# Experts ranked by their count of rows, 768 slots for the last three, and the weighting of scores behind the division

## The chip, the cores and the metric

The kernel runs on one core of a Trainium2 chip. The metric is device microseconds of one execution, lower is better. Three runs of the kernel before gave a median of 543.9 us (542.6 to 544.37).

## The reference

An attention with gates (a recurrence over 768 steps, for 4 batches and 8 heads of 40) gives 3072 rows of 320 numbers. These rows go to a layer of eight experts: each row to the two experts with the highest noisy logits, with the two weights of a softmax.

```python
for t in range(S):                       # S = 768
    m_new = np.maximum(f_gate[:, :, t] + m, i_gate[:, :, t])
    f_stab = np.exp(f_gate[:, :, t] + m - m_new)
    i_stab = np.exp(i_gate[:, :, t] - m_new)
    m = m_new
    C = f_stab[:, :, None, None] * C + i_stab[:, :, None, None] * np.einsum('bhd,bhe->bhde', vt, kt)
    n = f_stab[:, :, None] * n + i_stab[:, :, None] * kt
    denom = np.maximum(np.abs(np.einsum('bhd,bhd->bh', n, qt)[:, :, None]), 1.0)
    y[:, :, t] = sigmoid(o_gate[:, :, t]) * np.einsum('bhde,bhe->bhd', C, qt) / denom
x = y.transpose(0, 2, 1, 3).reshape(3072, 320)
noisy_logits = x @ w_gate + np.log1p(np.exp(x @ w_noise)) * noise
top2 = np.argpartition(-noisy_logits, 2, axis=1)[:, :2]
top2_w = softmax of the two
for e in range(8):
    for k in range(2):
        mask = top2[:, k] == e
        h = np.maximum(x[mask] @ w1[e], 0.0)          # 320 -> 1024
        out[mask] += top2_w[mask, k, None] * (h @ w2[e])   # 1024 -> 320
```

## The kernel before

**Attention.** The recurrence is computed in 24 units, each a chunk of 64 steps for two batches, 128 rows of the result. The order of the work on each engine is written out by hand. Unit `i` issues, among others: `s_part` (scores `s`, PE), `e_part` (the weights `w` from the gates), `k_part` (DVE: `kd`, the keys scaled for the state), `p_part` (DVE: `p` = `s` times `w`, 128 x 1024), `c_part` (PE: the new state `st`, ACT copies it), `o_part` (PE: `o` from `p` and the values and state), `f_part` (DVE: the reciprocal `dn` of the denominator, its maximum, then `tm` = `o` times `dn`; POOL: `xr` = `tm` times the output gate) and `l_part`, `t_part` (PE: logits and transposes). `k_part` and `p_part` prepare unit `i + 1` while unit `i` is still in its later steps; `p` and `kd` have two buffers each.

**Routing.** Behind each group of units the two best experts of its rows, the softmax weights, and the rank of each row within its expert are computed in fp32, mostly on DVE (`g_part`: `ln`, `na`, `co`, `m`, `mi`, and `ob`, a one-hot of the rank that PE adds into a table). `fill()` puts these small instructions between the attention's, so many per call. The table `TBL` has 7 columns per expert and 128 rows: slot `t * 128 + p` of expert `e` holds a row number (or nothing), with a sign that says which of the two weights is meant. `decode` turns columns of it into row numbers `TOK` and masks `KM`. POOL gathers rows by `TOK` (`gather`) and adds results back by it (`put`).

**Experts.** Every expert has room for 832 rows: six tiles of 128 and one of 64. The matrix products are done in parts of high and low precision (`w1h`, `w1l`, `xh`, `xl`, `hh`, `hlo`, ...). The first layer (`mm1`, L931) goes over 8 chunks of 128 hidden units, for each of two halves of the rows, 448 and 384 wide for experts 2 to 7; 8 matmuls per chunk. ACT and DVE turn each chunk into `hh` and `hlo`. The last 64 rows of the first half go to `ht` (L951). The second layer (`mm2`, L960 to L962) makes 24 matmuls per tile of 128 rows; the tile of 64 rows makes 16 (L968, L969). Expert 0 is done in three parts of rows, 0 to 384, to 640 and to 832, as routing finishes, beside the end of the attention; expert 1 in parts of 512 and 320.

While one expert computes, SP loads the next one's weights (`load_w1`, `load_w2`), ACT and DVE split them into high and low, POOL gathers the next rows, DVE turns them (`turn_x`), 16 DMAs on SP spread them over the partitions (`spread_x`), and `split_x` splits them. After expert 7 a flag is read: if any expert has more than 832 rows, a branch (`tc.If(most > NT)`) works through the rest.

The loop over the experts, with the places that the change touches:

```python
for h in range(2):
    for f in range(8):
        mm1(e, h, f)
        ...
        if TURN <= 8 * h + f < TURN + 7 and e + 1 < NE:
            turn_x(8 * h + f - TURN)
            if 8 * h + f == TURN + 6:
                spread_x()
                weigh(e + 1)
xs = split_x()
for n, t in enumerate(OR1):
    put(e, t, mm2(e, t))
```

Of the kernel before, what the change touches and what calls it, by code (L numbers as in the profile page):

```python
# [31 lines left out]
FIT = 2048  # L32
# [4 lines left out]
NB = 4  # L37

# [20 lines left out]
def build(ctx, tc, qk, vk, fi, noise, wgn, w1, w2, cst, ce, out):  # L59
# [30 lines left out]
    flag = keep.tile([128, 1], I32, name="flag")  # L90
    early = ctx.enter_context(tc.tile_pool(name="early", bufs=1))
# [43 lines left out]
    def load_w1(e, ks=((0, 2), 2)):  # L135
        for k in ks:
            if k == 2:
                for p in range(2):
                    SP.dma_start(RAW1[64 * p:64 * p + 64, 2], w1[e, 256:320])
            else:  # L140
                a, b = k
                SP.dma_start(RAW1[:, a:b], w1[e, a * 128:b * 128].rearrange("(k p) f -> p k f", p=128))
# [303 lines left out]

    def decode(a, b, more=True):

        t, n = TBL[:, a:b], slice(a, b)
        V.scalar_tensor_tensor(VC[:, n], t, 0.0, cs[:, C_VAC + a:C_VAC + b], op0=OP.is_equal, op1=OP.mult)  # L450
        V.scalar_tensor_tensor(AB[:, n], t, -1.0, t, op0=OP.mult, op1=OP.max)
        V.tensor_scalar(KM[:, n, 0], t, 0.0, None, op0=OP.is_gt)
        x = AB[:, n]
        if more:
            far = rt.tile([128, b - a], F32, name=f"far{a}", bufs=1)
            V.tensor_scalar(far, x, 0.5, FIT // 2, op0=OP.mult, op1=OP.add)
            x = rt.tile([128, b - a], F32, name=f"near{a}", bufs=1)
            V.scalar_tensor_tensor(x, AB[:, n], 0.0, far, op0=OP.add, op1=OP.min)
        V.scalar_tensor_tensor(TOK[:, n], x, -1.0, VC[:, n], op0=OP.add, op1=OP.add)
        V.tensor_scalar(KM[:, n, 1], t, 0.0, None, op0=OP.is_lt)  # L460
# [24 lines left out]
    def g_part(g):  # L485
# [121 lines left out]
        if u0 + nb == NU:  # L607
# [3 lines left out]
            yield  # L611
            V.tensor_reduce(dd[:, 0:1], rk[:, 0:8], AX.X, OP.max)
# [68 lines left out]
    def parts(e):  # L681
        s = (E0S, (0, 512, NT))[e] if e < 2 else (0, CA, NT)
        return [slice(a, b) for a, b in zip(s, s[1:])]


    def load_w2(e):
        SP.dma_start(RAW2, w2[e].rearrange("(j p) c -> p j c", p=128))
# [38 lines left out]
    def tiles(e, h=None):  # L726
        if h is None:
            return range(7)
# [22 lines left out]
    while i < NU - LEAD:  # L751
# [33 lines left out]
        p_part(i + 1)  # L785
# [11 lines left out]
        f_part(i, lambda: fill(0.15, False))  # L797
        t = l_part(i)
# [93 lines left out]
    QC = (224, 224, 192, 192)  # L892
    QO = (0, 224, 448, 640)
# [8 lines left out]
    def spread_x():  # L902
# [6 lines left out]
    def split_x():  # L909
# [88 lines left out]
    def advance(much, by=1):  # L998
# [61 lines left out]
    assert done[0] == NU  # L1060
    load_w2(1)
# [8 lines left out]
    for f in range(8):  # L1070
        mm1(0, 2, f)
        if f == 5:
            next(side)
        if f in (0, 3):
            transpose_x(tiles(0, 1)[f // 3])
    for t in tiles(0, 2):
# [9 lines left out]
    for e in range(1, NE):  # L1086
# [4 lines left out]
        for h in range(2):  # L1091
            for f in range(8):
# [7 lines left out]
                if TURN <= 8 * h + f < TURN + 7 and e + 1 < NE:  # L1100
                    turn_x(8 * h + f - TURN)
                    if 8 * h + f == TURN + 6:
                        spread_x()
# [11 lines left out]
        xs = split_x()  # L1115
        for n, t in enumerate(OR1):
# [45 lines left out]
    with tc.If(most > NT):  # L1162
        V.memset(ec, 0.0)
        with tc.For_i(0, NE, 1) as e:
            weights(e)
            x = xf[0:CS, 0:RW]
            tok = m2.tile([128, 1], I32, name="ftk")
            km = m2.tile([128, 2], F32, name="fkm")
            SP.dma_start(tok[0:CS], TOK[CS:128].rearrange("p (e c) -> p e c", e=NE)[:, bass.ds(e, 1), TC - 1:TC].rearrange("p e c -> p (e c)"))
            SP.dma_start(km[0:CS], KM[CS:128].rearrange("p (e c) k -> p e c k", e=NE)[:, bass.ds(e, 1), TC - 1].rearrange("p e k -> p (e k)"))  # L1170
            P.indirect_dma_start(out=x, out_offset=None, in_=XD, in_offset=bass.IndirectOffsetOnAxis(ap=tok[0:CS], axis=0),
# [106 lines left out]
```

## Time and profile before

| | |
|---|---|
| median of three runs | 543.9 us |
| profiled execution, span | 545.7 us |
| first matmul of expert 0 | at 138.6 us |
| matmuls (PE), share of the span | 96% |
| DVE, share of the span | 66% |
| ACT, POOL | 47%, 42% |

The page shows one profiled execution: busy time of each engine, then 40 slices of the span in tenths, the DMA queues, the chain that ended last, and groups of instructions. In a row of a group stands: line, engine, operation, `out<-in` by the program's names, shape, count, busy time in us, mean duration in ns, and behind the bar the engine's idle time just before such instructions, with what ended it. PE is TensorE's matmul, PEld its weight load, DVE VectorE, ACT ScalarE, POOL GpSimd, SP SyncE (it issues DMAs here). The expert stage takes the larger part of the span: an expert of 2 to 7 takes about 47.7 us.

### The profile page before, as it was taken

To read this page: it belongs to the slowest core of one execution; us is meant where nothing else is said; L and a number is where in the kernel's file an instruction comes from. 1 tells how busy PE (TensorE), PEld (TensorE's weight loads), DVE (VectorE), ACT (ScalarE), POOL (GpSimd) and SP (SyncE) were. 2 spreads that over 40 slices of the span, in tenths; PEclk is the share of its full clock that TensorE was granted. 3 is DMA by queue.
4 is the path that set the end of the run, shared out by engine and by line. 5 is a ranking of instruction groups with operands and counts; after the bars stand their busy time and mean duration, and the time that the engine had idled before them with its cause. 6 is when DMAs were issued, how large, how long until landed. Compare 5 with 4: busy or idle time off the path is not lost.

```text
span 545.7 us, 13298 instructions
## 1 busy us (share of the span) xinstructions
PE 521.9 (96%) x5100; PEld 486.9 (89%) x5101; DVE 361.6 (66%) x983; ACT 255.1 (47%) x634; POOL 227.9 (42%) x282
## 2 busy tenths in 40 slices
PE   8889998988999899999999999999999999999995
PEld 3778887877989798999999999999999999999994
DVE  8988999998786377764854675485467548546411
ACT  8858877877614154432541543254154325415300
POOL 7445463164112837056224705632570563251043
PEclk9979999998999999999999999999999999999998
DMA  5898787897767626088159418614941771461033
GB/s 147 216 229 221 205 227 189 199 223 197 264 191 236 106 41 194 10 170 225 39 97 261 93 35 231 136 47 81 270 97 31 194 171 49 92 144 21 1 36 47
DMA packets 49797, 77.25 MB, mean 142 GB/s; under 512 B 10281, under 2 KB 39664, under 8 KB 49728
## 3 DMA queue, kind: packets, MB, share of 16 engines
q1 hardware_dynamic: 38464, 57.39, 37.9%
q0 software_dynamic: 11264, 18.95, 19.0%
q8 instruction: 42, 0.69, 0.5%
q14 instruction: 27, 0.22, 0.1%
HBM read 52.49 MB, written 17.73 MB: 129 GB/s over the span
## 4 chain that ended last, share of the span: by engine, by line
PE 73%; DVE 20%; issue 2%; DMA 1%; ACT 1%; POOL 1%; POOLq 0%; DVEq 0%; SPq 0%; ACTq 0%
PE s L931 24%; PE e L931 12%; PE o L960 5%; PE o L961 5%; PE o L962 5%; PE st L961 5%; PE st L960 4%; PE st L962 4%; DVE p L348 3%; DVE ob L602 2%; DVE kd L342 2%; DVE tm L382 1%; PE o L371 1%; PE st L969 1%; PE st L968 1%
## 5 line engine op out<-in xcount | busy, mean ns | idle before, releaser
L983 POOL DMA_INDIRECT y_out<-y,tok x56 | 92.3, 1647 | 194.8 <-DVE y L973 191.2
L940 ACT ACTIVATE hh<-s 128x384 fp32r<-128x384 f32 (+3 forms) x91 | 42.7, 470 | 83.0 <-PE s L931 80.7
L931 PE MATMUL s<-xh,w1h 128*128 128x384 f32 (+5 forms) x273 | 78.6, 345 | 0.9 <-DVE xh L743 0.8
L709 POOL DMA_INDIRECT xg<-rows,tok x56 | 63.0, 1125 | 29.2 <-issue 15.1
L931 PE MATMUL s<-xh,w1l 128*128 128x384 f32 (+5 forms) x273 | 64.3, 343 | 0.6 <-DVE xh L743 0.6
L943 DVE SCALAR_TENSOR_TENSOR hlo<-s,hh 128x384 fp32r<-128x384 f32 (+3 forms) x91 | 47.5, 522 | 20.1 <-ACT hh L940 16.6
L961 PE MATMUL o<-w2l,hh 128*128 128x320 f32 x192 | 59.8, 311 | 0.0
L960 PE MATMUL o<-w2h,hh 128*128 128x320 f32 x192 | 59.7, 311 | 0.0
L962 PE MATMUL o<-w2h,hlo 128*128 128x320 f32 x192 | 59.1, 308 | 0.0
L931 PEld LDWEIGHTS s<-xh,w1h 128*128 128x128 f32 x273 | 49.2, 188 | 4.0 <-ACT hh L940 1.0
L961 PE MATMUL st<-w2l,hh 128*128 128x320 f32 x168 | 52.3, 311 | 0.3 <-issue 0.3
L960 PE MATMUL st<-w2h,hh 128*128 128x320 f32 x168 | 52.1, 310 | 0.0
L962 PE MATMUL st<-w2h,hlo 128*128 128x320 f32 x168 | 51.7, 308 | 0.0
L931 PEld LDWEIGHTS s<-xh,w1l 128*128 128x128 f32 x273 | 48.4, 188 | 3.2 <-DVE xh L743 0.9
L931 PE MATMUL s<-xl,w1h 128*128 128x384 f32 (+5 forms) x182 | 47.6, 343 | 0.0
L383 POOL TENSOR_TENSOR xr<-tm,vk 128x320 f32<-128x320 f32 x24 | 21.3, 887 | 52.9 <-DVE tm L382 10.6
L973 DVE TENSOR_SCALAR y<-o,gw 128x320 f32<-128x320 f32 x24 | 13.2, 550 | 42.3 <-PE o L962 42.3
L931 PE MATMUL e<-xh,w1h 128*128 128x384 f32 (+5 forms) x135 | 39.6, 348 | 0.4 <-DVE ht L951 0.3
L973 DVE TENSOR_SCALAR y<-st,gw 128x320 f32<-128x320 f32 x21 | 11.6, 551 | 41.2 <-PE st L962 41.1
L940 ACT ACTIVATE hh<-e 128x384 fp32r<-128x384 f32 (+3 forms) x45 | 21.3, 473 | 34.6 <-PE e L931 24.9
L960 PEld LDWEIGHTS o<-w2h,hh 128*128 128x128 f32 x192 | 36.1, 188 | 0.3 <-DVE y L973 0.2
L962 PEld LDWEIGHTS o<-w2h,hlo 128*128 128x128 f32 x192 | 36.2, 188 | 0.0
(222 smaller groups left out, 1303.3 us busy)
## 6 DMA issues: line engine op xcount, KB each, us to landing
vk<-vk_in SPq DMA_DIRECT2D x48, 242.0 KB
raw<-w_in SPq DMA_DIRECT2D x7, 1280.0 KB
qk<-qk_in SPq DMA_DIRECT2D x48, 160.0 KB
raw<-w_in SPq DMA_DIRECT2D x7, 1024.0 KB
raw<-w_in SPq DMA_DIRECT2D x19, 256.0 KB
y_out<-zrow SPq DMA_DIRECT2D x15, 320.0 KB
xt__2782<-xb SPq DMA_DIRECT2D x24, 84.0 KB
rows<-xr POOLq DMA_DIRECT2D x12, 160.0 KB
```

What stands on the lines that cost most here:

```text
L342: V.tensor_mul(KD[u], VKS[u % 4][:, :, 328:648].rearrange("p x (h d) -> p x h d", h=H), W[u][:, :, :, L - 1:L].to_broadcast([128, 2, H, D]))
L348: V.tensor_mul(PP[u], SQ[u], W[u])
L383: P.tensor_mul(XR[u], tm.rearrange("p h d -> p (h d)"), SG[u % 4])
L709: P.indirect_dma_start(out=XG[0:rows_of(t), t], out_offset=None, in_=XD[0:n], in_offset=bass.IndirectOffsetOnAxis(ap=token(e, t), axis=0), ...
L931: T.matmul(ps[:, 0:n], l, r, start=i == 0, stop=i == len(ops) - 1)
L940: A.activation(hi, x, AF.Relu)
L943: V.scalar_tensor_tensor(lo, x, 0.0, hi.bitcast(F32), op0=OP.max, op1=OP.subtract)
L960: T.matmul(ps, HH[:, j, c], W2H[:, j], start=j == 0, stop=False)
L961: T.matmul(ps, HH[:, j, c], W2L[:, j], start=False, stop=False)
L962: T.matmul(ps, HLO[:, j, c], W2H[:, j], start=False, stop=j == 7)
L973: V.tensor_scalar(y[0:n], ps[0:n], GW[e][0:n, t:t + 1], None, op0=OP.mult)
L983: st = P.indirect_dma_start(out=out, out_offset=bass.IndirectOffsetOnAxis(ap=token(e, t), axis=0), in_=y[0:n], in_offset=None, compute_op= ...
```

## The change

There are two parts.

First, experts 2 to 7 are worked through by falling count of rows. Six experts are ranked behind the last group's ranks: `key` = 8 times the count less the expert's number, `over` compares all pairs, its sum `POS` is the rank of each, `SEL` the one-hot of rank and expert, `WHO` the expert's number at each rank. `deal` multiplies the columns of `TBL` for these experts by `SEL` and adds over the experts, so that `TBP` holds the table in the order of ranks; it is then decoded. This is spread over the chunks of expert 0's third part. Weights of the expert at a rank are addressed with a number that SP loads from `WHO` into a register. The first three by rank keep 832 slots; the last three have 768, in halves of 384 and 384, six tiles and no `ht`. The flag takes another 64 on the count of these three, and the branch for what does not fit works on up to 128 rows left over per expert.

Second, `p_part(i + 1)` no longer stands right behind `k_part(i + 1)` but behind `f_part(i)`.

```diff
+    def deal():
+        x = rt.tile([128, NR, TC, NR], F32, name="dealt", bufs=1)
+        rows_ = TBL[:, EF * TC:].rearrange("p (e t) -> p t e", e=NR)
+        V.tensor_mul(x, SEL[:, :, None, :].to_broadcast([128, NR, TC, NR]), rows_[:, None].to_broadcast([128, NR, TC, NR]))
+        yield
+        V.tensor_reduce(TBP.rearrange("p (r t) -> p r t", r=NR), x, AX.X, OP.add)
+        yield
+        yield from decode_steps(EF * TC, NE * TC, True, TBP)
...
+            V.scalar_tensor_tensor(key, held, 8.0, i8[:, EF:8], op0=OP.mult, op1=OP.subtract)
+            V.tensor_tensor(over, key[:, None, :].to_broadcast(sq), key[:, :, None].to_broadcast(sq), op=OP.is_gt)
+            V.tensor_reduce(POS, over, AX.X, OP.add)
+            V.tensor_tensor(SEL, POS[:, None, :].to_broadcast(sq), i8[:, 0:NR, None].to_broadcast(sq), op=OP.is_equal)
+            V.tensor_mul(over, SEL, i8[:, None, EF:8].to_broadcast(sq))
+                V.tensor_reduce(WHO, over, AX.X, OP.add)
+            V.tensor_scalar(key, POS, LONG - 0.5, float(CS), op0=OP.is_gt, op1=OP.mult)
+            V.tensor_add(held, held, key)
...
-        s = (E0S, (0, 512, NT))[e] if e < 2 else (0, CA, NT)
+        s = (E0S, (0, 512, NT))[e] if e < EF else (0, CA, NT) if is_long(e) else (0, NM // 2, NM)
...
+    def weights_of(e):
+        if e < EF:
+            return slice(e, e + 1)
+        if e not in whose:
+            whose[e] = nc.values_load(WHO[0:1, e - EF:e - EF + 1], engines=[mybir.EngineType.SP], min_val=EF, max_val=NE - 1,
...
+        return bass.ds(whose[e], 1)
+
+    def is_long(e):
+        return e < EF + LONG
...
-            return range(7)
+            return range(7 if is_long(e) else 6)
...
         k_part(i + 1)
-        p_part(i + 1)
         fill(0.2, False)
         s_room(i + 2)
         c_part(i)
...
         f_part(i, lambda: fill(0.15, False))
+        p_part(i + 1)
         t = l_part(i)
...
-    QC = (224, 224, 192, 192)
-    QO = (0, 224, 448, 640)
+    def quarters(e):
+        return ((224, 224, 192, 192), (0, 224, 448, 640)) if is_long(e) else ((192,) * 4, (0, 192, 384, 576))
...
-                decode(E0S[h] // 128, E0S[h + 1] // 128 if h < 2 else NE * TC)
+                decode(E0S[h] // 128, E0S[h + 1] // 128 if h < 2 else EF * TC)
...
+    while routing:
+        fill(1.0)
+    dealing = deal()
...
     for f in range(8):
         mm1(0, 2, f)
+        next(dealing, None)
...
-                if TURN <= 8 * h + f < TURN + 7 and e + 1 < NE:
+                if e + 1 < NE and 8 * h + f - TURN in tiles(e + 1):
...
-        for n, t in enumerate(OR1):
+        xs = split_x(e + 1) if e + 1 < NE else iter(())
+        for n, t in enumerate(x for x in OR1 if x in tiles(e)):
```

On DVE, in one unit of the attention (a unit in the middle, with routing between its steps; `kd` and `p` are those of the next unit), the order before is:

```order
L342 TENSOR_TENSOR kd<-vk_108,w 128x640
L348 TENSOR_TENSOR p<-s,w 128x1024
L376 RECIPROCAL dn<-o 128x8
L503 SCALAR_TENSOR_TENSOR co_1804<-t_4_1741,ue_1740 128x32
L378 SCALAR_TENSOR_TENSOR dn<-dn 128x8
L505 RECIPROCAL na_1738<-t_4_1741 128x32
L382 SCALAR_TENSOR_TENSOR tm<-dn,o 128x320
L507 TENSOR_TENSOR co_1804<-co_1804,na_1738 128x32
L509 TENSOR_TENSOR ln_1742<-ln_1742,co_1804 128x32
```

and with the change, in the same unit:

```order
L350 TENSOR_TENSOR kd<-vk_112,w 128x640
L384 RECIPROCAL dn<-o 128x8
L534 SCALAR_TENSOR_TENSOR co_1806<-t_4_1745,ue_1744 128x32
L386 SCALAR_TENSOR_TENSOR dn<-dn 128x8
L536 RECIPROCAL na_1742<-t_4_1745 128x32
L390 SCALAR_TENSOR_TENSOR tm<-dn,o 128x320
L356 TENSOR_TENSOR p<-s,w 128x1024
L538 TENSOR_TENSOR co_1806<-co_1806,na_1742 128x32
L540 TENSOR_TENSOR ln_1746<-ln_1746,co_1806 128x32
```

`p` moves over the division's three instructions and the routing between them; the routing keeps its place among the rest, and now follows `p` where it followed `tm`.

On DVE, in the third part of expert 0 with the change (`dealt` and `tbp` are the dealing; `hlo`, `ht` are chunks of the first layer; `xl`, `xh` are rows of expert 1 being split):

```order
L1011 SCALAR_TENSOR_TENSOR hlo<-e,hh 128x128
L1019 SCALAR_TENSOR_TENSOR ht<-e,ht 128x64
L487 TENSOR_TENSOR dealt<-sel,tbl 128x252
L808 TENSOR_TENSOR xl<-s_3458,xh 128x2x128
L809 TENSOR_TENSOR xh<-s_3458,xh 64x128
L1011 SCALAR_TENSOR_TENSOR hlo<-s_3465,hh 128x128
L1019 SCALAR_TENSOR_TENSOR ht<-s_3465,ht 128x64
L489 TENSOR_REDUCE tbp<-dealt 128x42
```

Of these rows L487 and L489 are new; each of the dealing's instructions stands behind one chunk's `ht` and ahead of what follows it.

On SP, the loads of an expert's weights and the spreading of its rows, before:

```order
L687 DMA raw_2777<-w_in 128x8x320
L142 DMA raw_116<-w_in 128x2x1024
L139 DMA raw_116<-w_in 64x1024 x2
L907 DMA xt__2782<-xb 32x2x224 x2
L907 DMA xt__2782<-xb 32x3x224 x2
```

and with the change:

```order
L753 DMA raw_2781<-w_in 128x8x320
L745 TENSOR_LOAD who
L150 ISA
L150 DMA raw_120<-w_in 128x2x1024
L147 ISA
L147 DMA raw_120<-w_in 64x1024
L147 ISA
L147 DMA raw_120<-w_in 64x1024
L974 DMA xt__2786<-xb 32x2x224 x2
L974 DMA xt__2786<-xb 32x3x224 x2
```

The transfers stand in the same order; a register load from `who` and the arithmetic on addresses (ISA) come ahead of them.

More of the change, by code (lines that the diff above doesn't have):

```diff
@@ L37 @@
 NB = 4
+EF, LONG = 2, 3
+NR = NE - EF
 STEP, SHARE = 0.19, 1.65
@@ L90, in build @@
     flag = keep.tile([128, 1], I32, name="flag")
+    POS = keep.tile([128, NR], F32, name="pos")
+    WHO = keep.tile([128, NR], I32, name="who")
+    SEL = keep.tile([128, NR, NR], F32, name="sel")
+    TBP = keep.tile([128, NR * TC], F32, name="tbp")
     early = ctx.enter_context(tc.tile_pool(name="early", bufs=1))
@@ L445, in bc_part, with decoding @@
             done[0] += len(b[0]) // 2
-    def decode(a, b, more=True):
[L449 to L460, printed above, removed]
+    def decoding(t, vac, tok, km, vc, ab, more, pool, name):
+        V.scalar_tensor_tensor(vc, t, 0.0, vac, op0=OP.is_equal, op1=OP.mult)
+        yield
+        V.scalar_tensor_tensor(ab, t, -1.0, t, op0=OP.mult, op1=OP.max)
+        yield
+        V.tensor_scalar(km[:, :, 0], t, 0.0, None, op0=OP.is_gt)
+        yield
+        x = ab
+        if more:
+            shape = [128, ab.shape[1]]
+            far = pool.tile(shape, F32, name=f"far{name}", bufs=1)
+            V.tensor_scalar(far, x, 0.5, FIT // 2, op0=OP.mult, op1=OP.add)
+            yield
+            x = pool.tile(shape, F32, name=f"near{name}", bufs=1)
+            V.scalar_tensor_tensor(x, ab, 0.0, far, op0=OP.add, op1=OP.min)
+            yield
+        V.scalar_tensor_tensor(tok, x, -1.0, vc, op0=OP.add, op1=OP.add)
+        yield
+        V.tensor_scalar(km[:, :, 1], t, 0.0, None, op0=OP.is_lt)
+        yield
@@ new lines, in decode_steps @@
+    def decode_steps(a, b, more=True, t=None):
+        n = slice(a, b)
+        t = TBL[:, n] if t is None else t
+        return decoding(t, cs[:, C_VAC + a:C_VAC + b], TOK[:, n], KM[:, n], VC[:, n], AB[:, n], more, rt, a)
+    def decode(a, b, more=True):
+        run(decode_steps(a, b, more))
+    def deal():
+        x = rt.tile([128, NR, TC, NR], F32, name="dealt", bufs=1)
+        rows_ = TBL[:, EF * TC:].rearrange("p (e t) -> p t e", e=NR)
+        V.tensor_mul(x, SEL[:, :, None, :].to_broadcast([128, NR, TC, NR]), rows_[:, None].to_broadcast([128, NR, TC, NR]))
+        yield
+        V.tensor_reduce(TBP.rearrange("p (r t) -> p r t", r=NR), x, AX.X, OP.add)
+        yield
+        yield from decode_steps(EF * TC, NE * TC, True, TBP)
@@ L1075, in build @@
             transpose_x(tiles(0, 1)[f // 3])
+    run(dealing)
     for t in tiles(0, 2):
```

60 lines of the change are left out of this document (43 added, 17 removed).

## The prediction

> **What bounds the kernel now.** I read the page's busy shares and slices first, then the windows by stage, then the chain that ended last, and last the timelines of the two stages that the change touches.
>
> ```profile
> span 545.7 us, 13298 instructions
> PE 521.9 (96%) x5100; PEld 486.9 (89%) x5101; DVE 361.6 (66%) x983; ACT 255.1 (47%) x634; POOL 227.9 (42%) x282
> PE   8889998988999899999999999999999999999995
> DVE  8988999998786377764854675485467548546411
> PEclk9979999998999999999999999999999999999998
> ```
>
> The reader is to see two kernels in one. In the first ten slices (the attention) both PE and DVE stand near 9 tenths; from slice 15 on (the experts) PE alone is full. The windows put numbers to it (columns: length, busy PE, PEld, DVE, ACT, POOL, then clock, DMA share, GB/s).
>
> ```profile
> 45.00:125.00 80.00, 73.45 (x1746) 65.19 (x1744) 76.39 (x236) 63.42 (x171) 37.00 (x58) 1.00 0.84 212
> 139.00:205.00 66.00, 62.92 (x439) 57.34 (x438) 44.56 (x185) 25.49 (x76) 23.77 (x28) 1.00 0.60 164
> 205.00:539.00 334.00, 333.94 (x2009) 323.99 (x2007) 189.49 (x454) 122.96 (x303) 135.96 (x146) 1.00 0.48 112
> ```
>
> From 205 to 539 us PE is idle 0.06 us in 334, at full clock: what PE is spared there, the kernel is spared. From 45 to 125 us DVE is idle 3.6 us in 80 and PE 6.55: DVE sets the pace, but PE is only 6.55 us behind it, so a faster DVE can win at most that there. The chain confirms it: in the attention it runs on DVE nearly without a break.
>
> ```profile
> 86.07 0.73 DVE kd L342
> 86.80 1.14 DVE p L348
> ...
> 88.76 2.59 DVE ob L602 x4
> ```
>
> **Part 1, the last three experts: 768 slots for 832.** PE's timeline of expert 6 before (its first half of 448 columns, its second of 384, then the tiles of the second layer):
>
> ```profile
> 442.93 0.57 PE L931 MATMUL s<-xh,w1h 128*128 128x448 f32 x2
> ...
> 456.07 0.52 PE L931 MATMUL e<-xh,w1h 128*128 128x384 f32 x2
> ...
> 467.37 0.31 PE L960 MATMUL st<-w2h,hh 128*128 128x320 f32 x1
> ...
> 470.90 0.31 PE L968 MATMUL o<-w2h,ht 128*128 128x320 f32 x1
> ...
> 473.25 0.31 PE L960 MATMUL st<-w2h,hh 128*128 128x320 f32 x1
> ```
>
> Take the starts, not the durations, since matmuls overlap. Eight chunks of 448 columns take 456.07 - 442.93 = 13.14 us, eight of 384 take 467.37 - 456.07 = 11.30. With 768 slots both halves are 384 wide, so 1.84 us goes. The seventh tile, of 64 rows (L968, L969), takes 473.25 - 470.90 = 2.35 us and goes whole. That is 4.19 us an expert, **12.6 us** for three. Experts 2 to 4 keep their shape.
>
> PE must stay the bound in the shorter chunk of 1.41 us (11.30 / 8). DVE's work beside it:
>
> ```profile
> L943 DVE SCALAR_TENSOR_TENSOR hlo<-s,hh 128x384 fp32r<-128x384 f32 x56 | 30.4, 544 | 8.7 <-ACT hh L940 8.6
> L723 DVE TENSOR_TENSOR w2l<-raw,w2h 128x320 fp32r<-128x320 f32 x44 | 22.0, 500 | 6.7 <-ACT w2h L722 1.6
> ```
>
> 0.54 + 0.50 = 1.04 us a chunk; the small tile's pieces on ACT and DVE go too. The turning of the next expert's rows is spread over six steps, as now over seven. DVE has room. POOL loses one gather and one store per short expert, and SP keeps as many row-spreading DMAs, with fewer bytes.
>
> SP gains a register load of `who` and address arithmetic ahead of each weight load from expert 2 on. Behind it wait the weight loads and the spreading DMAs. No row before shows such a load feeding a DMA. A lower bound is 0, since SP waits anyway; an upper one is the 0.82 us that a whole weight-load issue takes:
>
> ```profile
> 240.80 0.82 SPq L142 DMA_DIRECT2D raw<-w_in  x1
> 270.62 0.62 ACT L149 ACTIVATE w1h<-raw 128x512 fp32r<-128x512 f32 x1
> ```
>
> These weights are issued at 240.80 and first used at 270.62, 29.8 us later; 0.82 us disappears in that cover, so I take 0. Were the cover gone, it would be at most 6 x 0.82 = 4.9 us.
>
> A rule speaks against this part. The row: 384 columns go at 11.30 / 64 = 177 ns per matmul, 448 at 205, at a granted clock of 1.00, so time follows the columns (0.46 ns each). The Trainium skill ("TensorE: Matmul & The Clock Gate", section "Back-to-back issue gap") says that in a stream of weight loads and matmuls the spacing is set by both, about 81 ns at 128 columns and 131 at 512; that is 0.13 ns a column, and by it the narrower half would bring an estimated 3 x 64 x 64 x 0.13 ns = 1.6 us, not 5.5. The rows contradict it here.
>
> **Part 2, ranking and dealing.** New on DVE: eight small instructions behind the last ranks, then a product of 252 elements, its sum to 42, and seven of 42, one per chunk of expert 0's third part, while the earlier decode shrinks from 51 columns to 9.
>
> ```profile
> 171.52 0.21 DVE L450 SCALAR_TENSOR_TENSOR vc<-tbl,cs 128x51 f32<-128x51 f32 x1
> 188.77 0.44 PE L931 MATMUL s<-xh,w1h 128*128 128x192 f32 x2 [0.78 <-DVE xh L743]
> 191.09 0.44 PE L931 MATMUL e<-xh,w1h 128*128 128x192 f32 x2 [0.33 <-DVE ht L951]
> ```
>
> Seventeen instructions at about 0.21 us are 3.6 us of DVE. DVE is idle 21 of 66 us in this stage, so most of it is hidden; but where PE already waits for DVE (188 to 192 us) it is not. Bounds: 0, and the ten dealing instructions at full price, 10 x 0.21 = 2.1, plus some 0.6 for a later gather behind three new instructions. I take **+1.0**, nearer the lower end, because DVE idles in a third of the stage. The gathers of expert 2 begin only at its predecessor's start, so the later decode of experts 2 to 7 delays nothing.
>
> **Part 3, the weighting `p` moves behind the division.** DVE runs the same instructions. What changes is what stands beside POOL's `xr`, which starts as soon as `tm` ends.
>
> ```profile
> 88.76 2.59 DVE L602 TENSOR_SCALAR ob<-spot,bi,cs 128x128 f16<-128x128 f16 x4
> 88.98 0.87 POOL L383 TENSOR_TENSOR xr<-tm,vk 128x320 f32<-128x320 f32 x1 [4.57 <-ACT w1h L129]
> 89.82 1.26 POOL L132 TENSOR_TENSOR w1l<-raw,w1h 128x512 fp32r<-128x512 f32 x1
> ```
>
> Four `ob` took 2.59 us beside POOL; a bare one takes 0.30. All routing instructions that fall there are stretched. Their least duration (first number of min/median/max) against their mean from 45 to 125 us:
>
> ```profile
> L509 DVE TENSOR_TENSOR ln<-ln,co x6: 193/848/1525, 52.5 to 150.0; 128x32 f32<-128x32 f32 x6
> L602 DVE TENSOR_SCALAR ob<-spot,bi,cs x48: 303/309/1430, 64.5 to 166.1; 128x128 f16<-128x128 f16 x48
> L348 DVE TENSOR_TENSOR p<-s,w x22: 1207/1218/1226, 17.7 to 133.0; 128x1024 f32<-128x1024 f32 x22
> ...
> L602 DVE TENSOR_SCALAR ob<-spot,bi,cs 128x128 f16<-128x128 f16 x24 | 9.7, 484 | 0.0
> L509 DVE TENSOR_TENSOR ln<-ln,co 128x32 f32<-128x32 f32 x4 | 4.1, 1018 | 0.4
> ```
>
> The two lose 24 x 0.181 + 4 x 0.825 = 7.6 us there (0.484 - 0.303 and 1.018 - 0.193 each), part of it to `w1l`. `p` never varies, also not where it runs beside an `xr`:
>
> ```profile
> 132.68 0.87 POOL L383 TENSOR_TENSOR xr<-tm,vk 128x320 f32<-128x320 f32 x1
> 133.04 1.23 DVE L348 TENSOR_TENSOR p<-s,w 128x1024 f32<-128x1024 f32 x1 [0.38 <-PE s L334]
> ```
>
> So `p` (1.22 us) can cover `xr` (0.87) whole. What is late next is PE. What PE has to win is its idle time ahead of `o`, which waits for `tm` now and will wait for `p`, at the same place in DVE's order:
>
> ```profile
> L371 PE MATMUL o<-vk,p 128*64 128x41 f32 (+2 forms) x491 | 17.5, 230 | 4.7 <-DVE tm L382 3.2 <-DVE mi L524 1.2 <-DVE co L507 0.3
> L376 DVE RECIPROCAL dn<-o 128x8 f32<-128x8 f32 x24 | 4.7, 197 | 2.0 <-PE o L371 2.0
> ```
>
> That is 4.7 us from 45 to 125 us (first row, that window). DVE's savings exceed it, so nearly all of it should go: **-4.5**. The new wait: the division no longer has `p` ahead of it and may wait for `o`; behind it stand `tm`, `p` and routing, and PE's next `o`. It waits 2.0 us in all 24 units now (second row, whole run), so there are few in which `o` is not done well before. At worst the division waits `p`'s 1.22 us longer in two or three of them, some 3 us, and PE and DVE both lose it. Bounds: +3 and -6.55; I take -4.5, the row's idle time less a little.
>
> **Sum.** -12.6 + 1.0 - 4.5 = -16.1 us against the profiled span of 545.7, hence 529.6 there. The median of the runs is 543.9, 1.8 us (0.3%) under that span; the difference carries over: **527.8 us**.
>
> **Rivals.**
>
> *A, the swap brings nothing.* DVE saves, but the division waits for `o` instead, and its wait takes the saving. It decides where the division comes to the head of DVE's queue before `o` has ended: `p` (1.22 us) no longer stands ahead of it there. For it: PE is busy 92% of that stage, so `o` is never much earlier than DVE needs it. Against it: the division waited for `o` only 2.0 us in 24 units although PE was as busy, and the routing that is moved ahead of it stays there. -12.6 + 1.0 = -11.6, so 532.3.
>
> *B, the swap brings all.* PE wins its whole 6.55 us between 45 and 125 us and another 1.0 in the units before and after, in which DVE also paces; dealing costs nothing. -12.6 - 7.6 = -20.2, so 523.7.
>
> *C, weight loads pace the narrower matmuls*, and in the three experts only the small tile goes: -3 x 2.35 - 4.5 + 1.0 = -10.6, so 533.3. It decides if a weight load takes as long as 448 columns do. The 384-wide chunks of before, at 1.41 us, speak against it. By the skill's figures in the sentence above, most of the first half's gain would be lost, which lies next to this case.
>
> *D, another stretch at half clock.* The windows around the first stretch of two in the attention:
>
> ```profile
> 27.30:40.90 13.60, 11.51 (x219) 10.29 (x218) 11.05 (x21) 7.22 (x18) 6.06 (x10) 0.75 0.91 230
> 34.00:40.60 6.60, 6.60 (x109) 6.03 (x108) 4.71 (x10) 3.66 (x9) 2.98 (x5) 0.50 0.92 241
> ```
>
> For 6.60 us the clock granted is 0.50, and PE is busy without a break: at full clock the same work takes 3.3 us, so a third such stretch costs up to 3.3, and one that goes wins as much. PE was idle 2.09 us in the 13.60 around it, hence a longer wait there decides it. With the swap, `o` waits less on average, which speaks for fewer; the division's own wait speaks for more. One more gives 531.1, one less 524.5.
>
> *E, the register holds up the weights.* SP stands still until `who` is loaded, and every split starts late. At the 0.82 us bound it isn't seen behind 29.8 us of cover; it decides only if the delay of each of six experts outgrows that cover by 2.7 us, 16.2 in all, and then the kernel comes out at 544.0, no change.
>
> *F, slower: the branch for overfull experts runs.* It stands behind `tc.If`, and the change adds 64 to the count of the three shortest, so one of them with more than 768 rows is enough to enter it. It then loads all weights again, one expert after the other, with PE waiting:
>
> ```profile
> raw<-w_in SPq DMA_DIRECT2D x7, 1280.0 KB
> raw<-w_in SPq DMA_DIRECT2D x7, 1024.0 KB
> GB/s 147 216 229 221 205 227 189 199 223 197 264 191 236 106 41 194 10 170 225 39 97 261 93 35 231 136 47 81 270 97 31 194 171 49 92 144 21 1 36 47
> ```
>
> An expert's weights are 1280 KB for the second layer and 1024 + 2 x 128 for the first, 2.6 MB; at the page's best slice of 270 GB/s that is 9.7 us, 78 for eight, and no slice shows more. 529.6 + 78 - 1.8 = about 606. Against it: drawing the reference's inputs and counting gives 742, 815, 769, 722, 783 and 752 rows for experts 2 to 7, hence 815, 783 and 769 for the long three, and 752, 742 and 722 for the short, all under 768. It decides only if the ranking picks others.
>
> **How the numbers follow.** The forecast, 527.8, has 0.64: its large term is read from starts on a full PE. A has 0.14, B 0.10, D 0.06 (half in either direction), C 0.02, E 0.02, F 0.02. The range must leave out no more than 2 in 10. The best ends of dealing (0) and of the swap (-6.55) give 524.7, the bad end of dealing (+2.7) gives 529.5. B at 523.7, A at 532.3, C at 533.3 and both of D are to lie inside; the swap's bad end (+3, 535.3) is left out with E and F. I take **522.5 to 534.0**. Two executions of this kernel differ by about 0.3%, so I call less than 1.6 us no change. Faster holds the forecast and A to D, 0.96; same E, 0.02; slower F, 0.02.
>
> **What would show it.** The terms in the order of their size, in the profile of the changed kernel:
>
> In the last three experts, the starts of the first matmuls of both halves stand 11.30 us apart from the next part, there is no tile of 64 rows, and the expert's period is 4.19 us shorter than that of the three before it, with PE still idle for less than 0.1 us from expert 2 on. If PE waits there, for DVE's `hlo` or for a split, the 12.6 is wrong. In the attention, `p` runs beside `xr` at its unchanged 1.22 us, `ln` and `ob` fall toward 193 and 303 ns, the idle time before `o` falls from 4.7 us toward nothing, and the first matmul of expert 0 starts about 4.5 us earlier. If the idle time before the division grows instead by several us, A is right. In expert 0's third part, PE's waits for `xh` and `ht` grow by about 1 us together. On SP, the row after the register load is a weight load issued at once, far ahead of its split. What would make the forecast wrong as a whole is a price in the attention beyond these bounds: a third stretch at 0.50, or DVE slowed by something else that POOL does beside routing.

## The result, and the profile after

| | before | changed |
|---|---|---|
| median, runs of the same job | 544.1 us (4 runs) | 529.9 us (4 runs) |
| ratio, 95% interval | | 0.970 (0.9653 to 0.9748) |
| profiled execution, span | 545.7 us | 530.0 us |

The change makes the kernel 3.0% faster by the ratio, 16.3 us of 544.1. The ratio is not the quotient of the two medians, which lie 14.2 us apart (2.6%); its interval holds both. The forecast was 527.8 us, 16.1 us less than before. The page of the changed kernel, in the parts that were shown of before: busy shares, slices, and the chain that ended last by engine.

```profile
span 530.0 us, 13180 instructions
PE 508.0 (96%) x5053; PEld 477.5 (90%) x5053; DVE 341.9 (65%) x964; ACT 249.6 (47%) x607; POOL 218.0 (41%) x273
PE   8979999998999889999999999999999999999995
DVE  8967989897788278773775385468437547645411
PEclk9979999997999999999999999999999999999999
PE 76%; DVE 12%; DMA 6%; issue 3%; POOL 1%; SPq 1%; ACT 1%; POOLq 0%; DVEq 0%
```

The reader is to see that the chain's share on DVE fell, from 20% to 12%, while PE's rose from 73% to 76% and that of transfers from 1% to 6%: DVE holds less of the attention. The windows by stage say the same (columns as before: length, busy PE, PEld, DVE, ACT, POOL, clock, DMA share, GB/s).

```profile
45.00:125.00 80.00, 76.04 (x1806) 67.55 (x1802) 72.52 (x246) 66.23 (x177) 37.98 (x60) 1.00 0.86 222
139.00:205.00 66.00, 62.06 (x433) 56.65 (x433) 47.23 (x199) 25.62 (x76) 24.01 (x27) 1.00 0.61 165
205.00:523.00 318.00, 318.00 (x1953) 312.54 (x1952) 177.91 (x413) 116.73 (x274) 125.64 (x136) 1.00 0.48 116
```

From 45 to 125 us PE was busy 73.45 us and DVE 76.39; now it is 76.04 and 72.52. The two have changed places, although the same 80 us now hold more of the work (246 instructions of DVE for 236). From 205 to 523 us PE is busy without a break.

Where the 15.7 us between the two spans came from, by the starts of the first matmul of each expert in PE's timeline:

| stretch | before | changed | difference |
|---|---|---|---|
| start to expert 0 | 138.62 | 136.94 | -1.68 |
| experts 0 and 1 | 112.63 | 112.85 | +0.22 |
| experts 2 to 4, each | 47.92 | 47.72 | -0.20 |
| experts 5 and 6, each | 47.92 | 43.49 | -4.43 |
| expert 7 and the end | 54.81 | 50.06 | -4.75 |

-1.68 + 0.22 - 3 x 0.20 - 2 x 4.43 - 4.75 = -15.67. PE's timeline of expert 6, to be held against the one of before:

```profile
436.43 0.51 PE L999 MATMUL s<-xh,w1h 128*128 128x384 f32 x2
...
447.61 0.51 PE L999 MATMUL e<-xh,w1h 128*128 128x384 f32 x2
...
458.79 0.31 PE L1028 MATMUL o<-w2h,hh 128*128 128x320 f32 x1
...
479.92 0.51 PE L999 MATMUL s<-xh,w1h 128*128 128x384 f32 x2
```

Both halves take 11.18 us, and behind the second come only tiles of 128 rows: the tile of 64 is gone. Two small things were not expected: 11.18 where a half of 384 columns took 11.30, and 0.20 us less in experts 2 to 4, whose shape is the same (before, an expert takes 47.92 us, not about 47.7 as stated ahead of the prediction). The second halves of experts 2 to 4 still take 11.30 us in the changed kernel, so the 0.12 belongs to the shorter shape; these are the starts of the two halves of expert 4 and of its second layer:

```profile
345.23 0.57 PE L999 MATMUL s<-xh,w1h 128*128 128x448 f32 x2
...
358.17 0.51 PE L999 MATMUL s<-xh,w1h 128*128 128x384 f32 x2
...
369.47 0.31 PE L1028 MATMUL st<-w2h,hh 128*128 128x320 f32 x1
```

In the shorter shape the second half begins 64 rows earlier. Whether that is the reason was not tried.

### The profile page after: what moved, and what is told of

Same layout as the page of the kernel before. It is cut to its first block, busy times and chain, and to the rows that moved or that the text cites. A ratio compares the mean times of both kernels' runs of the same rounds, so it can differ in the third digit from the quotient of the medians.

```text
span 530.0 us, 13180 instructions
## 1 busy us (share of the span) xinstructions
PE 508.0 (96%) x5053; PEld 477.5 (90%) x5053; DVE 341.9 (65%) x964; ACT 249.6 (47%) x607; POOL 218.0 (41%) x273
## 4 chain that ended last, share of the span: by engine, by line
PE 76%; DVE 12%; DMA 6%; issue 3%; POOL 1%; SPq 1%; ACT 1%; POOLq 0%; DVEq 0%
PE s L999 23%; PE e L999 11%; PE o L1028 5%; PE o L1029 5%; PE o L1030 5%; PE st L1029 5%; PE st L1030 5%; PE st L1028 5%; DMA qk<-qk_in 3%; PE o L379 3%; PE s L342 2%; DMA le<-hl 2%; DVE p L356 2%; PE st L370 1%; DVE ob L633 1%
## 5 line engine op out<-in xcount | busy, mean ns | idle before, releaser
L1051 POOL DMA_INDIRECT y_out<-y,tok x53 | 87.1, 1644 | 191.3 <-DVE y L1041 188.1
L775 POOL DMA_INDIRECT xg<-rows,tok x53 | 59.4, 1121 | 28.6 <-issue 14.2
L999 PE MATMUL s<-xh,w1l 128*128 128x384 f32 (+5 forms) x273 | 62.5, 336 | 0.7 <-DVE xh L809 0.7
L1029 PE MATMUL o<-w2l,hh 128*128 128x320 f32 x184 | 57.3, 312 | 0.0
L1028 PE MATMUL o<-w2h,hh 128*128 128x320 f32 x184 | 57.2, 311 | 0.0
L1030 PE MATMUL o<-w2h,hlo 128*128 128x320 f32 x184 | 56.6, 308 | 0.0
L1029 PE MATMUL st<-w2l,hh 128*128 128x320 f32 x176 | 54.9, 312 | 0.6 <-issue 0.6
L1028 PE MATMUL st<-w2h,hh 128*128 128x320 f32 x176 | 54.5, 310 | 0.0
L1030 PE MATMUL st<-w2h,hlo 128*128 128x320 f32 x176 | 54.1, 307 | 0.0
L1041 DVE TENSOR_SCALAR y<-o,gw 128x320 f32<-128x320 f32 x23 | 12.7, 551 | 42.0 <-PE o L1030 41.9
L379 PE MATMUL o<-vk,p 128*64 128x41 f32 (+2 forms) x768 | 29.3, 235 | 5.7 <-issue 3.5
```

The lines of the kernel that those rows point to most:

```text
L379: T.matmul(OQ[u][half[p], h, :], PP[u][n, p, h, :], VK[u % 4][p][n, h * 41:h * 41 + 41], start=True, stop=True)
L775: P.indirect_dma_start(out=XG[0:rows_of(t), t], out_offset=None, in_=XD[0:n], in_offset=bass.IndirectOffsetOnAxis(ap=token(e, t), axis=0), ...
L999: T.matmul(ps[:, 0:n], l, r, start=i == 0, stop=i == len(ops) - 1)
L1028: T.matmul(ps, HH[:, j, c], W2H[:, j], start=j == 0, stop=False)
L1029: T.matmul(ps, HH[:, j, c], W2L[:, j], start=False, stop=False)
L1030: T.matmul(ps, HLO[:, j, c], W2H[:, j], start=False, stop=j == 7)
```

## The experiments

The kernel before had medians from 543.1 to 547.8 us in the four jobs, so only ratios within a job are compared; they are turned into microseconds with that job's median of before.

### The parts alone

The first kernel is the one before with only `p` moved. The second is the changed kernel with `p` put back. The third is the second with 832 slots for all, so with ranks, dealing and the loads by register, but no smaller shape. The fourth is the changed kernel on the same chip.

```diff
 first, from before:
         k_part(i + 1)
-        p_part(i + 1)
...
         f_part(i, lambda: fill(0.15, False))
+        p_part(i + 1)
 second, from the changed kernel:
         k_part(i + 1)
+        p_part(i + 1)
...
         f_part(i, lambda: fill(0.15, False))
-        p_part(i + 1)
 third, from the second:
-EF, LONG = 2, 3
+EF, LONG = 2, 6
```

> The kernel before with only p moved behind the division. Theory 'forecast' (PE wins the idle time before o): 4.5 us faster than before, 0.992. Theory 'division waits' (DVE's saving is taken by a wait for o): within 0.5 us of before. Theory 'half price' (read from the trace of the changed kernel, where expert 0 starts 1.7 us earlier, with a longer pause of PE at 31 us among it): 1.5 to 3 us faster, idle time of DVE before the reciprocal more than 3 us above before.

> The changed kernel with p back behind kd: ranks, dealing and 768 slots alone. Theory 'forecast': -12.6 + 1.0 = 11.6 us faster than before, 0.979. Theory 'more than forecast' (from the traces: slots 12.7, first halves of experts 2 to 7 another 0.19 each, dealing +0.2): 13.5 us faster, 0.975. Then both together must differ from it by what the first run shows of the swap.

> As the run before, but all six ranked experts keep 832 slots: ranking, dealing and the loads by register without the smaller shape. Theory 'forecast': 1.0 us slower than before (ranks and dealing), the period of an expert 47.92 us as before. Theory 'more than forecast': about 0.8 us faster than before, the period of experts 2 to 7 47.72 us although their shape is the same. Theory 'register holds up the weights': clearly slower, PE idle before the first layers.

> The changed kernel once more on the same chip as the three parts. If the parts add up, its gain is that of the swap alone plus that of the experts alone within 1 us; forecast 16.1 us faster than before (0.970), by the medians so far 14.0 (0.974).

| kernel | median | ratio to before (546.4 us) | 95% interval |
|---|---|---|---|
| swap alone | 545.1 us | 0.9967 | 0.994 to 0.9993 |
| experts alone | 532.9 us | 0.977 | 0.9724 to 0.9816 |
| ranks, all with 832 | 546.4 us | 1.0003 | 0.9973 to 1.0032 |
| both | 531.0 us | 0.9735 | 0.9685 to 0.9786 |

What follows: the smaller shape alone is the second against the third, 0.977 / 1.0003 = 0.9767, or -12.7 us (some 3 to each side by the two intervals), as forecast (-12.6). The swap is worth 0.33% alone and 0.9735 / 0.977 = 0.9964 on top of the experts: -1.8 to -2.0 us, under half of the -4.5 forecast. It is not nothing by the first interval, which ends at 0.9993; the second difference alone, some 3.7 us to each side, could not tell. So the first run's theory 'half price' came true, its sign too: DVE's idle time before the reciprocal is 7.3 us in its trace, for 2.0 before. The experts alone are 12.6 us faster, between their two theories, and the parts add up within their intervals. The third kernel, with ranks and dealing, takes as long as the one before, also between its theories, and its experts 3 to 6 have the period of 47.72 us that the second one named. So its zero has two terms, as the next run shows.

### The 0.2 us per expert

The change's new tiles (`pos`, `who`, `sel`, `tbp`) stand ahead of the weights in memory and shift their addresses by 416 bytes. The run shifts them in the kernel before by an unused tile:

```diff
     flag = keep.tile([128, 1], I32, name="flag")
+    pad = keep.tile([128, 104], F32, name="pad")
+    V.memset(pad[:, 0:1], 0.0)
```

> The kernel before with one unused tile of 416 bytes a partition, as large as the change's new tiles, which puts the expert's weights (w1h, w1l, w2h, w2l) at the addresses that they have in the changed kernel; no other work. Theory 'place': the period of experts 2 to 6 falls from 47.92 to 47.72 us with the same 448 and 384 columns, about 1.2 us for six experts, 0.998. Theory 'ranking': the 0.2 us came from something else in the change, and the period stays 47.92 us.

Measured: 0.9964 (0.9936 to 0.9992) of before's 543.1 us, -2.0 us. PE's timeline of expert 4 in this kernel, the first matmuls of both halves and, one expert on, of expert 5:

```profile
339.57 0.36 PE L933 MATMUL s<-xh,w1h 128*128 128x448 f32 x1
...
352.52 0.51 PE L933 MATMUL s<-xh,w1h 128*128 128x384 f32 x2
...
387.29 0.36 PE L933 MATMUL e<-xh,w1h 128*128 128x448 f32 x1
```

The first half takes 352.52 - 339.57 = 12.95 us for 13.14 before, the expert 387.29 - 339.57 = 47.72 for 47.92, with no other work. The chip is not the cause: on the chip of the four runs above, the swap alone, whose tiles stand as before, has 47.92 us, and the other three have 47.72. So the place of the tiles is worth 0.2 us an expert, 1.2 us for six, and it is no merit of ranking. With 1.2 (by the trace) to 2.0 us (by the clock) taken off the third run above, ranks and dealing cost 1.4 to 2.1 us; the intervals of both runs, 0.3% to each side, lie on this, so that nothing is not excluded.

### What keeps the swap from its 4.5 us

The idle time before `o` and the price of POOL beside DVE, from the groups of the changed kernel between 45 and 125 us:

```profile
L379 PE MATMUL o<-vk,p 128*64 128x41 f32 (+2 forms) x535 | 19.3, 230 | 2.9 <-DVE p L356 1.9 <-issue 0.7 <-DVE rk L595 0.2
L633 DVE TENSOR_SCALAR ob<-spot,bi,cs 128x128 f16<-128x128 f16 x26 | 8.4, 390 | 0.0
L540 DVE TENSOR_TENSOR ln<-ln,co 128x32 f32<-128x32 f32 x4 | 0.8, 193 | 0.4
```

`ln` fell from 1018 to 193 ns, its least; `ob` from 484 to 390, as `w1l` on POOL still stands beside some of them. Whether DVE won what was forecast is read on the same work, from the start of `o` in unit 6 to that in unit 20, before and then changed:

```profile
48.58:120.62 72.04, 65.49 (x1563) 58.06 (x1557) 69.34 (x220) 56.77 (x153) 32.81 (x55) 1.00 0.82 210
```

```profile
48.93:117.44 68.51, 65.02 (x1562) 57.73 (x1556) 61.63 (x217) 56.51 (x153) 32.84 (x54) 1.00 0.84 219
```

It did: DVE's busy time fell by 7.7 us. But the stretch is only 3.5 us shorter, PE's idle time before `o` between 45 and 125 us fell only from 4.7 to 2.9 us, and `p` ends most of it. The waits of DVE, before (first row) and then changed, between 45 and 125 us (us in total, times, longest):

```profile
DVE co L503 <- ACT t L642: 0.2, 1, 0.2
```

```profile
DVE co L534 <- ACT t L695: 2.6, 2, 1.4
DVE dd L585 <- ACT d L695: 1.4, 2, 0.8
DVE dn L384 <- PE o L379: 0.3, 1, 0.3
```

DVE has a new wait of 4.0 us there, for ACT. The wait that was named, of the division for `o`, is small in this window but not in the whole run:

```profile
L384 DVE RECIPROCAL dn<-o 128x8 f32<-128x8 f32 x24 | 4.8, 200 | 8.2 <-PE o L379 7.9
```

Before, it was 2.0 us. In the six traces of kernels with the swap in all units and the routing in its place it is 3.8 to 8.5 us, mean 7.0; in the five without the swap 0.7 to 2.8, mean 1.8. In the changed kernel it stands in the first and the last units, and the section on PE's pauses comes back to it. First the wait for ACT, in DVE's timeline of the changed kernel in unit 6:

```profile
50.14 0.21 DVE L384 RECIPROCAL dn<-o 128x8 f32<-128x8 f32 x1
51.74 0.19 DVE L534 SCALAR_TENSOR_TENSOR co<-t,ue 128x32 f32<-128x32 f32 x1 [1.40 <-ACT t L695]
51.85 0.16 DVE L386 SCALAR_TENSOR_TENSOR dn<-dn 128x8 f32<-128x8 f32 x1
...
52.19 0.43 DVE L390 SCALAR_TENSOR_TENSOR tm<-dn,o 128x320 f32<-128x320 f32 x1
52.53 1.21 DVE L356 TENSOR_TENSOR p<-s,w 128x1024 f32<-128x1024 f32 x1
```

The routing's `co`, which stands between the reciprocal and `dn`, needs `t`, which ACT makes of an exponential and has not finished yet. Before, `p` stood ahead and gave ACT 1.2 us. Now DVE stands, and `dn`, `tm` and `p` behind it. The next run moves these two steps of routing behind `p`, which gives ACT its time back; the run after it keeps the swap to units 6 to 19, because the first six and the last three units did not gain in the first traces; and the changed kernel runs beside them.

```diff
 routing behind p, from the changed kernel:
-        f_part(i, lambda: fill(0.15, False))
+        f_part(i, lambda: None)
         p_part(i + 1)
+        for _ in range(2):
+            fill(0.15, False)
 swap only there, from the changed kernel:
         k_part(i + 1)
+        if not 6 <= i < 20:
+            p_part(i + 1)
...
         f_part(i, lambda: fill(0.15, False))
-        p_part(i + 1)
+        if 6 <= i < 20:
+            p_part(i + 1)
```

> The changed kernel, but the two steps of routing that stood between the division's instructions stand behind p. Theory 'routing waits for ACT' (co and dd wait 2.6 and 1.4 us for ACT between 45 and 125 us, ahead of dn, tm and p): the wait before co falls below 1 us or no longer lies ahead of tm and p, PE's idle time before o in units 6 to 20 falls from 2.9 to under 2 us, and those units take 67.5 us for 68.5; 0.998 of both together. Theory 'DVE paces by its sum': 68.5 us as now, the wait only stands elsewhere. Theory 'bare division' (its three small instructions now stall on each other): slower, 0.2 us a unit, 4.8 us.

> The changed kernel with p behind the division only while units 6 to 19 are worked through; the units before and after have the order of before. Theory 'the order costs the early and late units' (with the swap the first six take 0.45 us more, the last three 1.1 more): first six 32.7 us, last three 15.4 us, 1.5 us faster than both together, 0.997. Theory 'PE's pauses' (PE paces there in either order, so a pause of it counts whole): the same as both together within 0.5 us, and the last three still take 1 us more than before where the pause of 1.7 us falls in unit 21.

> The changed kernel on the same chip as the two variants, to compare them with: 0.970 to 0.975 of before.

Measured: routing behind `p` 0.9721 (0.9676 to 0.9767), swap in units 6 to 19 0.9708 (0.9668 to 0.9747), both together 0.9706 (0.966 to 0.9752); medians 530.2, 530.5 and 530.2 us. The three times are equal, as far as intervals of some 2.5 us to each side can tell. The second variant had the wait of the division down to 2.8 us, and its first six and last three units at 32.4 and 14.8 us in the trace, as its first theory had it; the clock shows nothing of the 1.5 us. The first variant did to the waits what it was to do, but units 6 to 20 took 69.5 us in its trace, not 67.5. Its waits of DVE and its row of `o`, between 45 and 125 us:

```profile
DVE dn L384 <- PE o L379: 4.7, 6, 1.8
```

```profile
L379 PE MATMUL o<-vk,p 104*64 104x41 f32 (+2 forms) x512 | 18.0, 230 | 0.7 <-issue 0.6
```

DVE waits for ACT no more, and PE for `p` no more. Instead DVE now waits 4.7 us for PE: there PE is the bound. Three more runs, on the chip of the moved tiles:

> Ranks, dealing and 768 slots without the swap, on the same chip as both together. Theory 'forecast': 4.5 us above both together. Theory 'given back to PE' (1.8 us so far): 1 to 3 us above. Start of expert 0 later than with the swap by as much.

> The changed kernel beside the three others: 0.970 to 0.9735 of before.

> The changed kernel with the two steps of routing behind p. Theory 'PE is the bound now': DVE's wait for ACT ahead of p is gone and PE's idle time before o for p too, but PE's own pauses count whole, so the time is that of both together within 1 us. Theory 'routing waits for ACT takes the rest': 1.5 us under both together.

| kernel | median | ratio to before (543.1 us) | 95% interval |
|---|---|---|---|
| experts alone | 528.4 us | 0.9715 | 0.9674 to 0.9756 |
| both | 526.2 us | 0.968 | 0.9642 to 0.9718 |
| both, routing behind `p` | 527.0 us | 0.9689 | 0.9654 to 0.9724 |

The swap is worth 0.968 / 0.9715 = 0.9964 again, 2.0 us; both together came out a little under the ratio that was expected (0.970). Moving routing brings nothing that can be measured, 0.8 us slower in the first comparison and 0.5 in the second, with some 3 us to each side. Its traces agree: units 6 to 20 took 69.5 and 70.2 us, for 68.5 to 70.0 with the swap and routing in place. So "routing waits for ACT" is a wait that is there but not what holds the rest. No kernel here is measurably faster than the changed one.

### PE's pauses

What takes PE's time in that window? In the changed kernel's PE timeline, and in the one of before, unit 21:

```profile
126.56 0.90 PE L402 MATMUL xt<-cs,xr 128*128 128x128 f32 x3 [1.67 <-issue]
```

```profile
129.49 0.86 PE L394 MATMUL xt<-cs,xr 128*128 128x128 f32 x3 [1.74 <-issue]
```

PE stands for 1.7 us at the same instruction in both, and no other engine and no transfer of the program's data ends the pause ("issue"). DVE's timeline just after it, changed and then before (its `p` of before, with 0.38 us, is in the prediction's rows):

```profile
130.15 1.23 DVE L356 TENSOR_TENSOR p<-s,w 128x1024 f32<-128x1024 f32 x1 [1.79 <-PE s L342]
132.91 0.21 DVE L384 RECIPROCAL dn<-o 128x8 f32<-128x8 f32 x1 [1.53 <-PE o L379]
```

```profile
134.62 0.21 DVE L376 RECIPROCAL dn<-o 128x8 f32<-128x8 f32 x1 [0.35 <-PE o L371]
```

Before, DVE was late there, so the pause cost it 0.38 + 0.35 us; now it costs 1.79 + 1.53. A DVE that is late hides pauses of PE; one that is on time does not. The division's 7.9 us in the changed kernel are for the most part such waits: 2.86 us in unit 3, at a pause of PE of 2.78 us, 3.21 in unit 4, after the half clock that follows this pause (the granted clock is 0.50 from 34.0 to 40.5 us), and the 1.53 of unit 22 above.

```profile
33.11 0.38 PE L379 MATMUL o<-vk,p 128*64 128x41 f32 x7 [2.78 <-issue]
```

```profile
33.86 0.21 DVE L384 RECIPROCAL dn<-o 128x8 f32<-128x8 f32 x1 [2.86 <-PE o L379]
41.33 0.21 DVE L384 RECIPROCAL dn<-o 128x8 f32<-128x8 f32 x1 [3.21 <-PE o L379]
```

From the start of `o` in unit 20 to that in unit 23, five kernels without the swap (before, experts alone twice, ranks with 832, moved tiles) took 14.2 to 16.0 us, mean 15.2, and six with it 14.5 to 17.5, mean 15.9; from unit 6 to 20, 70.7 to 73.8, mean 71.8, against 68.5 to 70.0, mean 69.0. So the gain lies in units 6 to 20, 2.8 us of it, and less than nothing comes from the rest, though there the scatter is as large as the difference. In sum the traces agree with the clock: expert 0 starts at 135.7 us in the mean of five with the swap (the sixth has more work at its start) and at 137.5 in that of the five without.

The last run asks what such a pause belongs to. It computes 72 short matmuls more at the start that no result uses, in place of 8 long ones that none uses either:

```diff
-    warm(WARM)
+    warm(WARM - 8)
+    wq = psum.tile([128, 512], F32, name="o")
+    for _ in range(72):
+        T.matmul(wq[:, 0:32], wz[:, 0:128], wz[:, 0:32], start=True, stop=True)
```

> The changed kernel with 8 of the first 16 warming matmuls replaced by 72 short ones, so that PE has 128 instructions more ahead of unit 0; nothing else is computed. PE's pauses 'issue' of 1.4 to 2.8 us stood so far at its instructions 960, 1216, 1472 and 5056, which are 256 apart or multiples of it apart. Theory 'the pause belongs to the count' (PE's next instructions arrive late): pauses stand at the same counts and so 128 instructions earlier in the program, the one at 126 us no longer ahead of the transposes of unit 20 but about half a unit before. Theory 'the pause belongs to the work': it stays ahead of the same transposes at the count 5184.

Two of its three pauses in PE's timeline, in unit 4 and unit 22; the third, of 0.91 us, stands in unit 8:

```profile
36.85 1.17 PE L370 MATMUL st<-vk,kd 104*40 104x41 f32 x32 [1.87 <-issue]
...
132.84 0.36 PE L370 MATMUL st<-vk,kd 128*40 128x41 f32 x9 [1.30 <-issue]
```

These two stand at other work now (the state `st`). Counted over PE's instructions in the trace, weight loads included, the three stand at 1217, 2241 and 5313, as those of the other kernels do at 960, 1216, 1472, 3520 and 5056 (one more where the trace has a record more): always 192 above a multiple of 256. That holds for all 34 pauses "issue" of over 0.8 us in the attention of the fourteen traces; shorter ones stand elsewhere too. The pause belongs to the count. The expectation was right in the step of 256 but not in each count: 960, 1472 and 5056 passed without a pause this time, and 2241 and 5313 had one. Which of these counts shows a pause changes from run to run.

What PE waits for there is in the traces too. Among the DMA queues of the changed kernel's page is one for instructions (packets, MB, share of 16 engines):

```profile
q8 instruction: 42, 0.69, 0.6%
```

Its packets, by their times in the trace, have 16,384 bytes each and go with PE's count, one for each step of 256. The third of the changed kernel starts at 30.64 us and has landed at 31.73; PE goes on at 33.11, at the count 960. The nineteenth starts at 123.98 and has landed at 125.07; PE goes on at 126.56, at 5056. All 34 pauses end 1.3 to 1.8 us after the landing of the packet that belongs to their count. Of the first 21 packets of the fourteen traces, 294 in all, none landed less than 1.26 us before PE passed its count. Where no pause stands, half of them landed some 2.9 us or more ahead. So the theory that PE's next instructions arrive late holds. Why some of these packets start late is not shown.

## Why the prediction was right in sum, and where it was not

**The small shape, -12.6.** Right, nearly step by step. Held against the longer experts of the changed kernel itself, the narrower half brings 12.94 - 11.18 = 1.76 us (forecast 1.84), the tile 2.35 as forecast, and the other half 0.12 that was not in the sum: 4.23 us an expert, 12.7 for three; the runs give 12.7. PE stayed full, DVE, POOL and SP were no bound. A chunk of 384 columns takes 11.18 / 8 = 1.40 us, one of 448 12.94 / 8 = 1.62. The Trainium skill ("TensorE: Matmul & The Clock Gate", section "Back-to-back issue gap") has spacings by which the narrowing would bring an estimated 1.6 us for three experts. Here it is 3 x (12.94 - 11.18) = 5.3, which bears out the rows of before and not that estimate. Rival C is out.

**The register.** Right at 0. The weights of an expert stay issued 28.6 us ahead, as these two rows of the changed kernel show (SP's timeline, then ACT's):

```profile
240.38 0.38 SPq L150 DMA_DIRECT2D raw<-w_in  x1
```

```profile
268.97 0.63 ACT L157 ACTIVATE w1h<-raw 128x512 fp32r<-128x512 f32 x1
```

The six register loads of the changed kernel, with their durations in ns (least, median, longest):

```profile
L745 SPq TENSOR_LOAD <-who x6: 272/383/1110, 171.1 to 423.6; - x6
```

The longest, 1.1 us, is over the 0.82 us that was taken as an upper bound, and disappears in the 28.6 us all the same. Rival E is out, and F with it: the time shows no branch of 78 us.

**Ranks and dealing, +1.0.** In its bounds (0 to 2.7), with 1.4 to 2.1 us by the runs after the moved tiles are taken off. The working has a slip, nine dealing instructions and not ten, which lowers the upper bound to 2.5. The step "about 0.21 us each" was mis-sized for the large two of the new instructions, whose rows in the changed kernel's DVE timeline are

```profile
188.83 0.61 DVE L487 TENSOR_TENSOR dealt<-sel,tbl 128x252 f32<-128x252 f32 x1
190.84 0.41 DVE L489 TENSOR_REDUCE tbp<-dealt 128x42 f32<-128x252 f32 x1
```

and PE does wait where it was feared: 0.73 us for a matmul at 192.11 us, behind the decode. But its waits for DVE in the third part, 1.27 us in all before, are 1.53 now, 0.26 more, since that for `xh` got shorter. Where the rest of the 1.4 to 2.1 us lies, if there is one, the traces don't show.

**The swap, -4.5.** Mis-sized: -1.9 us by three pairs of runs. What it said of DVE was right: 7.7 us won on the same work, where 7.6 were counted, `p` at its 1.22 us beside `xr`, `ln` at its least. The step that failed is "DVE's savings exceed it, so nearly all of it should go", together with the new wait, "some 3 us" at worst. Of PE's 4.7 us before `o` only 1.8 went. The division's wait for `o`, 2.0 us before, grew by 5.9 us in the changed kernel and to a mean of 7.0 in six traces: the 2.0 us of before were read as `o` being done early, though `p` stood ahead of the division in every unit and covered 1.22 us. A wait that grows so is the sign that the prediction gave for rival A, and A's mechanism is at work, in the first and the last units above all, but it does not take the whole gain: A (nothing) is out by the first run's interval, which ends just under 1, and B (all) by its other end, as 0.994 is 3.3 us and B asked for 7.6. The new wait of DVE for ACT, 4.0 us, was not foreseen, but taking it away gave no time back that could be measured. With DVE on time PE is the bound for much of the attention, and its late instructions and half clock then show in DVE's waits. That these pauses are what holds the rest was seen in units 3, 4 and 22 and in DVE's wait for PE; it was not tried to take the pauses away, so how much of the missing 2.6 us is theirs stays open. Rival D cannot be told from the scatter: in the attention the granted clock stood at 0.50 for 10.2 us before and 13.7 us in the changed kernel, but for 6.8 to 13.7 us in the five traces without the swap and 0 to 13.7 in the nine with it.

**What was not in the sum.** The moved tiles bring 1.2 us by the trace, 2.0 (0.4 to 3.5) by the clock. That made up for about half of what the swap lacked. Summed up: 12.7 for the shape, 1.9 for the swap, and nothing for ranks, dealing and moved tiles together, is 14.6 us; both together gave 14.5 to 17.4 in the four jobs, each with an interval of some 2.5 to each side. The forecast of 16.1 came as near as it did partly by luck: two errors had opposite signs.

**The step from the span to the median.** It took the profiled 545.7 us as 1.8 above the median. In every run that gave both, a time is 1.8 us more than its span (531.83 for 530.0), so the profiled execution of before stands for a time of 547.5, some 3.6 us above the median that it was set beside. The forecast of the difference does not hang on this step; the two sides of it were not what was said.

## What to carry to other kernels

Where two engines are both near 9 tenths, the gap between them is an upper end for what relief of the one brings, not the expected value: the other's own pauses, which the slower one hid, come to light with it. A wait that is short now says little about a place from which the work ahead of it is taken away: look at what that work covered. Shortening the work of an engine that is full from first to last is worth the difference of the starts, to a tenth of a microsecond. When an instruction is moved, look also at who used the time it took: here ACT worked on `t` for the routing under it.

## What the runs showed of the hardware

PE's instructions come in packets of 16,384 bytes through a DMA queue, one for each 256 of them. In the attention PE pauses for up to 3.2 us at its instructions 192 above a multiple of 256 where such a packet is late: in 34 of 34 pauses of over 0.8 us PE goes on 1.3 to 1.8 us after the packet has landed. In the experts no such pause stands. Two things differ there: the transfers' share, 0.84 and 0.86 for 0.48 in the windows above, and PE's pace, by these windows an estimated 5.7 us for 256 instructions (3608 in 80 us) against 21 us in the experts (3905 in 318). Which of them makes the packets late in the attention was not tried.

Half clock can follow such a pause. Two windows of the changed kernel, the pause and what came after it:

```profile
124.90:126.55 1.65, 0.00 (x0) 0.00 (x0) 1.51 (x5) 0.78 (x2) 0.00 (x0) 0.86 1.05 249
126.60:132.50 5.90, 5.90 (x103) 5.33 (x104) 2.99 (x6) 4.01 (x9) 3.40 (x3) 0.50 0.62 157
```

After 1.65 us without work the granted clock is 0.50 for 5.90 us. It isn't so behind each pause: of the 34, 11 have a stretch at 0.50 that begins between their start and 2 us after their end, and in its first trace the kernel with routing behind `p` had four pauses of 1.2 to 2.4 us and a granted clock of 1.00 throughout the attention. Of the 25 stretches at 0.50 in the fourteen traces, the end of each run left out, the other 14 begin behind no such pause. The Trainium skill ("TensorE: Matmul & The Clock Gate", section "What's actually happening") puts the cold state behind an idle window of about 3.4 us. In this row PE was idle for half of that.

The same matmul of 448 columns came every 205 ns with its weights at one address and every 202 ns with them 416 bytes further on (13.14 and 12.95 us for 64). Which part of the address does it was not tried.
